# Row maxima with five PSUM banks and a priority of their own, and output tiles completed in turn, in a planned attention and feed-forward kernel

## The chip, the cores and the metric

The kernel runs on one core of one Trainium2 chip. The metric is the device time of one execution in microseconds, given as the median of several runs.

## What is computed

The reference is a decay attention followed by two feed-forward layers, all in float32:

```
B, H, S, D = 4, 8, 576, 64
scores = q @ k.T / 8 + (cum[:, None] - cum[None, :])     # cum = cumsum(log(clip(f, 1e-4, 1)))
scores = where(causal, -1e9, scores)
attn = exp(scores - rowmax(scores)); attn = attn / (sum(attn) + 1e-9)
x = (attn @ v), heads side by side                       # 2304 x 512
h = x @ w_in;  g = h * sigmoid(1.702 * h);                x = g @ w_out     # 512 -> 2048 -> 512
h = x @ w_in2; g = max(h, 0) + alpha * min(h, 0);         out = g @ w_out2  # 512 -> 2048 -> 512
```

## The kernel before, in words

**An order that a planner writes.** The function does not issue instructions directly. It hands operations to a planner (class `Plan`, lines 71 to 178): each with the engines that may run it and an assumed duration on each, the buffers that it reads and writes, and a priority. The method `run` keeps its own clock for every engine, for the SP and ACT DMA queues and for every buffer. In each step it takes, among all operations that can be placed, the one that can start earliest by that clock; among those with the same start the one with the lowest priority number, then the one that ends first, then the one added first:

```
if best is None or (t, o.pri, end, o.seq) < best[0]:
    best = ((t, o.pri, end, o.seq), o, eng, port)
```

The instructions are then issued in this order. On the chip each engine works through its own list in order, so an instruction whose operand is late holds up all that is behind it on that engine.

**Buffers.** A `Pool` has a number of slots, and an operation that writes a new buffer cannot be placed before a slot is free. All eight PSUM banks are one shared set (`all_banks`); each use of PSUM has a pool with a limit on how many of them it may hold at once (lines 307 to 311):

- `ps_s`, 4: attention scores. Each key tile takes two, one for each of two heads.
- `ps_m`, 2: the score tiles from which row maxima are taken, and the bank that transposes the maxima.
- `ps_v`, 3: the attention outputs. Each unit takes two.
- `ps_h` and `ps_y`, 2 each: hidden layer and output of the feed-forward blocks that run beside attention. `ps_h2` and `ps_y2`, 4 each, serve the later blocks.

**Attention** is cut into 32 units: two heads of one batch and one of two ranges of query rows (0 to 256, then 256 to 576). First come the 16 units of the first range, then the 16 of the second. A unit i has three parts.

- `prep` (line 500) loads k, q and v, transposes k and q on DVE (L518) and splits them into a high and a low part (L354 or L356, L359). Its priority is 100 + i - 2, so the preparation of unit i+2 has the priority 100 + i.
- `chunk` (line 572) finds the row maxima. For every tile of 128 query rows it multiplies q and k for each head (L602; the last 64 rows go by L595 and L596), adds the mask and takes the maximum on DVE (L611), merges two maxima for the last rows (L618), turns the maxima with a matmul against the identity (L627) and writes them with a minus sign into DQ (L636 on ACT or L638 on DVE). Priority 100 + i.
- `chunk2` (line 643) computes the scores again, key tile by key tile, in four products for each head. The last of them (DQ with DK) subtracts the maximum and adds the decay (L663). Then come the exponential on ACT (L667), the triangle on POOL (L671) and the product with the values (L683, L689, or L712 with split operands), and at the end the normalisation: L722 or L725, L728, L731, L732, L742. Priority 100 + i. It is added to the plan after `chunk` of the next unit.

The units of the first range have two key tiles, those of the second five.

**Feed-forward beside attention.** As soon as 256 columns of the attention output are there, `mlp1a` (line 776) runs the first 8 of 16 slices of the first layer on them (L755, L761, L762, L797), with priority 1000 and more, as filler for PE. The weights are split numbers that are put together on ACT, DVE and POOL first (`convert`, L475 to L489).

**Later blocks.** After attention the other 8 slices run in blocks of 512 columns (L755, L878), then the second layer (L755, L766, L769, L907) in five blocks, the last with 512 rows. A slot of the second layer first makes the hidden slice, splits it into gh and gl, and then adds the products for all four output tiles of 128 rows: gh for the four tiles (eight matmuls), then gl for the four tiles (four matmuls). After the last slot each tile is copied out of PSUM into a `qyp` buffer, of which there are two, and stored (L916, L921):

```
for t in range(nt):
    yo = Buf(q_yp)
    plan.add([("ACT", ...), ("DVE", ...)], ... copy(e, yo.ap, py[t].ap), [py[t]], [yo], base)
```

The copies show up under the lines of the helper, L354 and L356. `q_xb` is a pool of two buffers of the same shape, into which the blocks' inputs are loaded (`load_x`, line 857).

Of the kernel before, what the change touches and what calls it, by code (L numbers as in the profile page):

```python
# [181 lines left out]
def kernel(  # L182
# [20 lines left out]
    NP = H // 2  # L203
    KT = DM // P
    NM = DFF // P
# [12 lines left out]
    A0 = 100.0  # L218
    plan = Plan()
# [82 lines left out]
    def psum_pool(cap):  # L302
        p = Pool(cap, (), all_banks)
        p.make = lambda i: banks[i]
        return p

    ps_s = psum_pool(4)
    ps_m = psum_pool(2)
    ps_v = psum_pool(3)
    ps_h = psum_pool(2)  # L310
    ps_y = psum_pool(2)

# [5 lines left out]
    q_xb = sb("b1", "qxb", 2, [P, 512], F32, after_att)  # L318
    q_yp = sb("b1", "qyp", 2, [P, 512], F32, after_att)
# [23 lines left out]
    def c_dve(n, fast=False):  # L343
        return n / (1.92 if fast else 0.96) + 68.0

    def c_act(n, ps=False):
        return n / 1.2 + (51.0 if ps else 93.0)
# [56 lines left out]
    for nm, p, view, n, val in (  # L404
# [8 lines left out]
        for i in range(p.n):  # L413
            b = fill[nm, i] = Buf()
# [16 lines left out]
    for part, (lo, hi) in enumerate(((0, SPLIT), (SPLIT, S))):  # L431
        ts_ = [t for t in range(NKT) if lo <= t * P < hi]
        pri = -80 if part == 0 else A0 + 4.5
# [63 lines left out]
    W1, W2 = {}, {}  # L497
# [67 lines left out]
    def col0(b, q0):  # L565
        return b * SPLIT if q0 == 0 else B * SPLIT + b * (S - SPLIT)


    def c_mm(n, m=P):
        return max(0.4375 * n + 7.0, 111.0 if m > 64 else 57.0)  # L570

    def chunk(u, q0, q1, pri):
        kh, dk, qh, dq, z = u["kh"], u["dk"], u["qh"], u["dq"], u["z"]
        mx = Buf(p_mx)
        fmx = filled("mx", p_mx)
# [2 lines left out]
        nt = len(tiles)  # L578
# [45 lines left out]
        for i0 in range(0, len(jobs), 4):  # L624
# [5 lines left out]
            for i, (j, t, a, w, hhs) in enumerate(jb):  # L630
                for g, hh in enumerate(hhs):
# [6 lines left out]
                            nc.vector.tensor_scalar_mul(d, s_, -1.0)  # L638

                    plan.add([("ACT", 280.0), ("DVE", 240.0)], ev, [(pt, i0), *u["fdq"]], [(dq, ("x", i0 + i, hh))], pri)  # L640
        return dict(u=u, q0=q0, q1=q1, pri=pri)

    def chunk2(x):
        u, q0, q1, pri = x["u"], x["q0"], x["q1"], x["pri"]
# [182 lines left out]
    pend = []  # L827
    for i, (b, hp, q0, q1) in enumerate(seq):
        unit = prep(b, hp, q0, q1, A0 + i - PRE, i < EARLY, 2 <= i < ACTQ)
        pend.append((chunk(unit, q0, q1, A0 + i), col0(b, q0) + q1 - q0 if hp == NP - 1 else 0))  # L830
        if i == NP:
            for m in range(NA):
                W1[m] = weight(wA, w1_in, w1_out, m, A0 + 4 + m * 0.6, A0 + 1 + m if m < 2 else None)
        if len(pend) > 1:
            x, t = pend.pop(0)
            chunk2(x)
            advance(t, 0)
# [7 lines left out]
    blocks = []  # L845
# [21 lines left out]
    for i, (t0, n) in enumerate(blocks):  # L867
        base = 3000.0 + 100 * i
        rd = [(b_xs, c) for c in range(t0 // BLK, (t0 + n) // BLK)]
        xh, xl, rx = load_x(xscr, rd, t0, n, base - 150)  # L870
        py = [Buf(ps_y2) for _ in range(KT)]
        for m in range(NA, NM):
            gh, gl = mlp_slot(W1[m], xh, xl, rx, n, ps_h2, q_g, "swish", m, base + m, base + m - 50)

            def ymm(e, i_, m=m, gh=gh, gl=gl, py=py, n=n):
                for d in range(KT):
                    for a, g in ((0, gh), (1, gh)) if i_ == 0 else ((0, gl),):
                        nc.tensor.matmul(  # L878
                            py[d].ap[:, :n], W1[m].ap[:, a, KT + d, :], g.ap[:, :n],
                            start=(m == NA and i_ == 0 and a == 0), stop=(m == NM - 1 and i_ == 1),  # L880
                        )
# [13 lines left out]
    for i, (t0, n) in enumerate(blocks):  # L895
        base = 4000.0 + 100 * i
        xh, xl, rx = load_x(y1scr, [(b_y1, (i, d)) for d in range(KT)], t0, n, base - 150)
        nt = n // P
        py = [Buf(ps_y2) for _ in range(nt)]
        for m in range(NM):  # L900
            gh, gl = mlp_slot(W2[m], xh, xl, rx, n, ps_h2, q_g, "prelu", m, base + m, base + m - 50)

            def ymm(e, i_, m=m, gh=gh, gl=gl, py=py, nt=nt):
                wo = W2[m].ap.rearrange("p a c n -> p a (c n)")
                for t in range(nt):
                    for a, g in ((0, gh), (1, gh)) if i_ == 0 else ((0, gl),):
                        nc.tensor.matmul(  # L907
                            py[t].ap, g.ap[:, t * P:(t + 1) * P], wo[:, a, KT * P:],
                            start=(m == 0 and i_ == 0 and a == 0), stop=(m == NM - 1 and i_ == 1),
                        )  # L910

            plan.add([("PE", 2 * nt * c_mm(512))], lambda e, ymm=ymm: ymm(e, 0), [(W2[m], (1, 0)), (W2[m], (1, 1)), gh], py, base + m)
            plan.add([("PE", nt * c_mm(512))], lambda e, ymm=ymm: ymm(e, 1), [(W2[m], (1, 0)), gl], py, base + m)
        for t in range(nt):
            yo = Buf(q_yp)
            plan.add([("ACT", c_act(512, True)), ("DVE", c_dve(512))], lambda e, t=t, yo=yo, py=py: copy(e, yo.ap, py[t].ap), [py[t]], [yo], base)  # L916
            x = t0 + t * P
            while x < t0 + (t + 1) * P:
                r, y = row_of(x)
                y = min(y, t0 + (t + 1) * P)  # L920
                plan.add(DMA((y - x) * 2048), lambda e, x=x, y=y, r=r, yo=yo, o=x - t0 - t * P: nc.sync.dma_start(  # L921
                    out[r:r + y - x, :], yo.ap[o:o + y - x, :]
                ), [yo], (), base)
                x = y
# [37 lines left out]
```

## Time and profile before

| | |
|---|---|
| median of 3 runs | 1076.21 us (1075.81 to 1078.11) |
| the profiled execution | 1075.87 us, span 1074.1 us |
| PE matmul busy | 1033.8 us, 96% of the span |
| PE weight load busy | 886.3 us, 83% |
| DVE busy | 690.3 us, 64% |
| ACT busy | 447.9 us, 42% |
| POOL busy | 125.5 us, 12% |
| DMA | 86.55 MB, mean 81 GB/s |

Times count from the start of the span. PE, DVE, ACT, POOL and SP are the engines. A row of the timeline gives the start, the duration, the engine, the line of the kernel, what is written from what, and how many instructions were merged; in square brackets stands how long the engine had been idle and what ended that. An arrow points from the one who waited to what it waited for. Attention ends at about 418 us, and the feed-forward work beside it at about 480 us.

### The profile page before, as it was taken

To read this page: it belongs to the slowest core of one execution; us is meant where nothing else is said; L and a number is where in the kernel's file an instruction comes from. 1 tells how busy PE (TensorE), PEld (TensorE's weight loads), DVE (VectorE), ACT (ScalarE), POOL (GpSimd) and SP (SyncE) were. 2 spreads that over 40 slices of the span, in tenths; PEclk is the share of its full clock that TensorE was granted. 3 is DMA by queue.
4 is the path that set the end of the run, shared out by engine and by line. 5 is a ranking of instruction groups with operands and counts; after the bars stand their busy time and mean duration, and the time that the engine had idled before them with its cause. 6 is when DMAs were issued, how large, how long until landed. Compare 5 with 4: busy or idle time off the path is not lost.

```text
span 1074.1 us, 17787 instructions
## 1 busy us (share of the span) xinstructions
PE 1033.8 (96%) x6531; PEld 886.3 (83%) x6531; DVE 690.3 (64%) x1565; ACT 447.9 (42%) x1042; POOL 125.5 (12%) x192
## 2 busy tenths in 40 slices
PE   5868999999999899999999999999999999999997
PEld 3656888889998789998878898888888888898885
DVE  5879987888878877959963359734343533534433
ACT  4557554665555565847742247301211201211101
POOL 6223221211111111002100101200000000000000
PEclk7789999999999999999999999999999999999999
DMA  5577563333242111645742235300200200000001
GB/s 110 120 172 183 128 154 73 67 78 66 48 92 41 52 24 60 215 140 175 227 159 88 79 118 177 118 1 1 69 1 1 69 0 1 33 28 20 1 1 39
DMA packets 170056, 86.55 MB, mean 81 GB/s; under 512 B 127440, under 2 KB 155280, under 8 KB 169968
## 3 DMA queue, kind: packets, MB, share of 16 engines
q1 hardware_dynamic: 160720, 84.30, 28.8%
q10 hardware_dynamic: 9248, 1.12, 0.7%
q8 instruction: 51, 0.84, 0.3%
q14 instruction: 37, 0.30, 0.1%
HBM read 66.34 MB, written 19.02 MB: 79 GB/s over the span
## 4 chain that ended last, share of the span: by engine, by line
PE 51%; DVE 3%; DMA 2%; ACT 1%; issue 0%; SPq 0%; DVEq 0%; ACTq 0%
PE bk L755 26%; PE bk L907 18%; PE bk L878 6%; DMA wraw<-in_moe_w_out_dram 1%; PE bk L797 1%; DVE wraw L484 1%; DVE wA L359 1%; DVE wc L487 0%; DVE qgg L762 0%; ACT wraw L480 0%; DVE qgl L359 0%; ACT wc L479 0%; DMA qxb<-xscr 0%; DVE wc L481 0%; DMA out_dram<-qyp 0%
## 5 line engine op out<-in xcount | busy, mean ns | idle before, releaser
L354 ACT CAST qgh<-qgg 128x512 fp32r<-128x512 f32 (+1 forms) x118 | 68.2, 578 | 334.3 <-DVE qgg L769 297.3
L766 DVE TENSOR_SCALAR qgg<-bk,alpha_sb 128x512 f32<-128x512 f32 (+1 forms) x80 | 55.4, 694 | 164.9 <-PE bk L755 164.9
L755 PE MATMUL bk<-qx,wB 128*128 128x512 f32 (+1 forms) x720 | 155.8, 368 | 0.0
L755 PEld LDWEIGHTS bk<-qx,wB 128*128 128x128 f32 x720 | 125.9, 189 | 22.7
L755 PE MATMUL bk<-xh,wA 128*128 128x256 f32 x576 | 120.6, 292 | 0.0
L359 DVE TENSOR_TENSOR qgl<-qgg,qgh 128x512 fp32r<-128x512 f32 (+1 forms) x117 | 74.8, 641 | 68.8 <-ACT qgh L354 52.2
L755 PE MATMUL bk<-qx,wA 128*128 128x512 f32 (+1 forms) x480 | 103.6, 368 | 0.0
L755 PEld LDWEIGHTS bk<-xh,wA 128*128 128x128 f32 x576 | 95.3, 192 | 7.0 <-issue 4.0
L755 PEld LDWEIGHTS bk<-qx,wA 128*128 128x128 f32 x480 | 84.2, 188 | 15.3
L797 PE MATMUL bk<-gh,wA 128*128 128x256 f32 x576 | 82.9, 287 | 3.9 <-ACT gh L354 3.2
L755 PE MATMUL bk<-xl,wA 128*128 128x256 f32 x288 | 81.9, 284 | 1.1 <-DVE xl L359 1.1
L611 DVE CUSTOM_DVE_ANT_0 bk<-bk,mask 128x512 f32<-128x512 f32 (+3 forms) x160 | 75.2, 492 | 10.1 <-PE bk L602 8.3
L797 PEld LDWEIGHTS bk<-gh,wA 128*128 128x128 f32 x576 | 73.8, 191 | 7.6 <-ACT gh L354 3.9
L667 ACT ACTIVATE e<-bk 128x320 f32<-128x320 f32 (+3 forms) x224 | 66.5, 364 | 22.4 <-PE bk L663 21.4
L907 PE MATMUL bk<-wA,qgh 128*128 128x512 f32 x288 | 71.9, 389 | 0.0
L907 PEld LDWEIGHTS bk<-wA,qgh 128*128 128x128 f32 x288 | 53.8, 188 | 11.0
L671 POOL TENSOR_SCALAR_AFFINE_SELECT e<-e 128x256 f32<-128x256 f32 (+1 forms) x80 | 33.6, 432 | 208.4 <-ACT e L667 180.6
L755 PEld LDWEIGHTS bk<-xl,wA 128*128 128x128 f32 x288 | 55.4, 192 | 1.4 <-DVE xl L359 1.3
L878 PE MATMUL bk<-qgh,wB 128*128 128x512 f32 (+1 forms) x240 | 54.3, 368 | 0.8 <-ACT qgh L354 0.8
L907 PE MATMUL bk<-wB,qgh 128*128 128x512 f32 x216 | 53.9, 390 | 0.0
L479 ACT ACTIVATE wc<-wraw 128x512 f32<-128x512 f32 x64 | 43.1, 678 | 24.3 <-DMA wraw<-in_moe_w_out_dram 11.8
L755 PE MATMUL bk<-qx,wC 128*128 128x512 f32 (+1 forms) x240 | 52.8, 368 | 0.0
(154 smaller groups left out, 2038.4 us busy)
## 6 DMA issues: line engine op xcount, KB each, us to landing
wraw<-in_moe_w_in_dram SPq DMA_DIRECT2D x32, 512.0 KB
wraw<-in_moe_w_out_dram SPq DMA_DIRECT2D x32, 512.0 KB
xscr<-xr SPq DMA_DIRECT2D x9, 512.0 KB
ypscr<-yp SPq DMA_DIRECT2D x18, 256.0 KB
rk<-in_k_dram SPq DMA_DIRECT2D x64, 72.0 KB
VR<-in_v_dram SPq DMA_DIRECT2D x32, 128.0 KB
qxb<-xscr SPq DMA_DIRECT2D x16, 256.0 KB
qyp<-ypscr SPq DMA_DIRECT2D x16, 256.0 KB
```

The costliest lines, as they stand in the source:

```text
L354: nc.scalar.copy(dst, src)
L359: E[e].tensor_tensor(dst, a, b, op=ALU.subtract)
L479: plan.add([("ACT", c_act(n))], lambda e: nc.scalar.mul(w.ap, high().bitcast(F32), 2.0 ** -112), [raw], [w], pri)
L484: lambda e: nc.vector.scalar_tensor_tensor(low(), high(), -2 ** 31, low(), op0=ALU.bitwise_and, op1=ALU.bitwise_or),
L611: plan.add([("DVE", c_dve(c1 - c0) + 90.0)], lambda e, pm=pm, c0=c0, c1=c1, mk=mk, m0=m0, col=col: nc.vector.tensor_tensor_reduce(pm.ap[:, ...
L667: plan.add([("ACT", c_act(m, True))], lambda e, hh=hh, pss=pss, e32=e32, w=w, m=m: nc.scalar.activation(e32.ap[:w, hh, :m], pss[hh].ap[:w, ...
L671: plan.add([("POOL", 150.0 + 0.82 * 2 * w, 0.0, True)], lambda e, e32=e32, w=w: nc.gpsimd.affine_select(e32.ap[:w, :, :w], e32.ap[:w, :, : ...
L755: nc.tensor.matmul(ph.ap[:, :n], wb.ap[:, a, c, :], x(c), start=(c == 0 and i == 0), stop=(c == KT - 1 and i == 2))
L766: plan.add([("DVE", c_dve(n) + 56)], lambda e: nc.vector.tensor_scalar(g.ap[:, :n], ph.ap[:, :n], 0.0, alpha_sb[:, m:m + 1], op0=ALU.min, ...
L797: nc.tensor.matmul(py[d // 2].ap[:, d % 2 * BLK:(d % 2 + 1) * BLK], W1[m].ap[:, a, KT + d, :], g.ap, start=(m == 0 and i == 0 and a == 0 a ...
L878: nc.tensor.matmul(py[d].ap[:, :n], W1[m].ap[:, a, KT + d, :], g.ap[:, :n], start=(m == NA and i_ == 0 and a == 0), stop=(m == NM - 1 and ...
L907: nc.tensor.matmul(py[t].ap, g.ap[:, t * P:(t + 1) * P], wo[:, a, KT * P:], start=(m == 0 and i_ == 0 and a == 0), stop=(m == NM - 1 and i ...
```

## The change

Three things change.

- The limits on PSUM banks: scores 4 to 2, maxima 2 to 5, attention outputs 3 to 4. The eight banks stay shared.
- The operations of `chunk` get the priority 100 + i - 0.5 instead of 100 + i. `chunk2` and `prep` keep theirs.
- In the last slot of the last block the products of the output tiles are separate operations: gh for tiles 0 and 1, gl for tile 0, gl for tile 1, then gh and gl for tile 2, then gh and gl for tile 3, each with a slightly higher priority number than the one before. Tiles 1 and 3 of that block are copied into `qxb` buffers, tiles 0 and 2 into `qyp` buffers.

```diff
-    ps_s = psum_pool(4)
-    ps_m = psum_pool(2)
-    ps_v = psum_pool(3)
+    ps_s = psum_pool(2)
+    ps_m = psum_pool(5)
+    ps_v = psum_pool(4)
...
-    def chunk(u, q0, q1, pri):
+    def chunk(u, q0, q1, upri, pri):
...
-        return dict(u=u, q0=q0, q1=q1, pri=pri)
+        return dict(u=u, q0=q0, q1=q1, pri=upri)
...
-        pend.append((chunk(unit, q0, q1, A0 + i), ...))
+        pend.append((chunk(unit, q0, q1, A0 + i, A0 + i - 0.5), ...))
...
-            def ymm(e, i_, m=m, gh=gh, gl=gl, py=py, nt=nt):
+            def ymm(e, i_, m=m, gh=gh, gl=gl, py=py, ts_=range(nt)):
...
-                for t in range(nt):
+                for t in ts_:
...
-            plan.add([("PE", 2 * nt * c_mm(512))], lambda e, ymm=ymm: ymm(e, 0), [(W2[m], (1, 0)), (W2[m], (1, 1)), gh], py, base + m)
-            plan.add([("PE", nt * c_mm(512))], lambda e, ymm=ymm: ymm(e, 1), [(W2[m], (1, 0)), gl], py, base + m)
+            last = i == len(blocks) - 1 and m == NM - 1
+            for ts_ in (range(0, 2), range(2, 3), range(3, nt)) if last else (range(nt),):
+                k_ = len(ts_)
+                py_ = [py[t] for t in ts_]
+                plan.add([("PE", 2 * k_ * c_mm(512))], lambda e, ymm=ymm, ts_=ts_: ymm(e, 0, ts_=ts_), [(W2[m], (1, 0)), (W2[m], (1, 1)), gh], py_, base + m + 0.01 * ts_[0])
+                for t2 in ([t] for t in ts_) if last else (ts_,):
+                    plan.add([("PE", len(t2) * c_mm(512))], lambda e, ymm=ymm, t2=t2: ymm(e, 1, ts_=t2), [(W2[m], (1, 0)), gl], [py[t] for t in t2], base + m + 0.01 * t2[0])
         for t in range(nt):
-            yo = Buf(q_yp)
+            yo = Buf(q_xb if last and t % 2 else q_yp)
```

## Rows read from the trace of the kernel before

**Rows 1.** The page: engine totals, and PE's busy share in 40 slices.

```profile
PE 1033.8 (96%) x6531; PEld 886.3 (83%) x6531; DVE 690.3 (64%) x1565; ACT 447.9 (42%) x1042; POOL 125.5 (12%) x192
...
PE   5868999999999899999999999999999999999997
```

**Rows 2.** Windows: length, busy PE, PEld, DVE, ACT, POOL; PEclk, DMA share, GB/s.

```profile
10.00:70.00 60.00, 42.71 (x302) 34.55 (x303) 44.41 (x150) 28.24 (x75) 19.94 (x32) 0.69 0.60 133
70.00:110.00 40.00, 34.05 (x296) 27.40 (x294) 38.38 (x110) 32.51 (x82) 12.47 (x17) 1.00 0.73 187
110.00:350.00 240.00, 239.71 (x2113) 213.04 (x2110) 200.93 (x553) 134.37 (x385) 40.65 (x68) 1.00 0.38 81
350.00:400.00 50.00, 46.82 (x401) 40.98 (x400) 40.52 (x112) 27.66 (x80) 5.89 (x11) 0.97 0.15 41
400.00:1060.00 660.00, 658.84 (x3384) 562.90 (x3383) 359.02 (x627) 215.99 (x411) 37.63 (x33) 1.00 0.23 72
```

**Rows 3.** Waits of PE over the whole span: total us, times, longest us.

```profile
PE bk L663 <- DVE DQ L638: 6.4, 1, 6.4
...
PE bk L627 <- DVE MX L611: 4.2, 1, 4.2
...
PE bk L627 <- DVE MX L618: 2.5, 2, 2.2
PE bk L663 <- ACT e L667: 2.4, 3, 1.5
...
PE bk L602 <- DVE MX L611: 0.8, 1, 0.8
```

**Rows 4.** Timeline of the end; last row: the output stores, ns min/median/max.

```profile
1063.53 0.69 DVE L359 TENSOR_TENSOR qgl<-qgg,qgh 128x512 fp32r<-128x512 f32 x1 [0.76 <-ACT qgh L354]
...
1063.68 1.98 PE L907 MATMUL bk<-wC,qgh 128*128 128x512 f32 x8
...
1065.49 1.07 PE L907 MATMUL bk<-wC,qgl 128*128 128x512 f32 x4
1065.92 0.59 ACT L354 COPY qyp<-bk 128x512 f32<-128x512 f32 x1 [2.43 <-PE bk L907]
...
1066.53 4.36 SPq L921 DMA_DIRECT2D out_dram<-qyp x5
1068.65 0.59 ACT L354 COPY qyp<-bk 128x512 f32<-128x512 f32 x1 [2.14 <-DMA out_dram<-qyp]
1069.95 0.59 ACT L354 COPY qyp<-bk 128x512 f32<-128x512 f32 x1 [0.71 <-DMA out_dram<-qyp]
...
L921 SPq DMA_DIRECT2D out_dram<-qyp x5: 333/338/587, 1066.5 to 1070.6; - x5
```

**Rows 5.** Timeline of 365 to 369 us, three operations of DVE.

```profile
365.68 0.51 DVE L518 STREAM_TRANSPOSE tq<-rq 128x320 f32<-128x320 f32 x1
...
367.73 0.77 DVE L518 STREAM_TRANSPOSE tk<-rk 128x576 f32<-128x576 f32 x1
...
368.52 0.10 DVE L618 TENSOR_TENSOR MX<-MX 128x1 fp32r<-128x1 f32 x1
```

**Rows 6.** Timeline of 14 to 15 us, DVE ahead of the first maxima.

```profile
14.71 0.51 DVE L462 CAST xr<-xr 32x320 fp32r<-32x320 f32 x1 [3.04 <-ACT xr L461]
```

**Rows 7.** Timeline of 62 to 64 us, ACT.

```profile
62.74 0.66 ACT L479 ACTIVATE wc<-wraw 128x512 f32<-128x512 f32 x1 [4.09 <-DMA wraw<-in_moe_w_in_dram]
...
63.97 0.27 ACT L636 ACTIVATE DQ<-bk 3x128 fp32r<-3x128 f32 x1
```

**Rows 8.** Timeline of 39 to 41 us: scores of two key tiles, exponentials.

```profile
39.17 0.33 PE L663 MATMUL bk<-QH,KH 64*128 64x256 f32 x2
...
39.69 0.28 PE L663 MATMUL bk<-QH,KH 64*128 64x128 f32 x1
...
39.98 1.19 ACT L667 ACTIVATE e<-bk 128x256 f32<-128x256 f32 x4 [0.15 <-PE bk L663]
```

**Rows 9.** Groups of PE's instructions, 10 to 110 us: busy us, mean ns | idle before.

```profile
L627 PE MATMUL bk<-ident_r,MX 128*99 128x128 f32 x10 | 3.4, 336 | 4.7 <-DVE MX L611 4.2 <-DVE sm L728 0.5
```

More of the change, by code (lines that the diff above doesn't have):

```diff
@@ L829 @@
         unit = prep(b, hp, q0, q1, A0 + i - PRE, i < EARLY, 2 <= i < ACTQ)
-        pend.append((chunk(unit, q0, q1, A0 + i), col0(b, q0) + q1 - q0 if hp == NP - 1 else 0))
+        pend.append((chunk(unit, q0, q1, A0 + i, A0 + i - 0.5), col0(b, q0) + q1 - q0 if hp == NP - 1 else 0))
         if i == NP:
```

## The prediction

> **What bounds the kernel now.** I read the page's engine totals and slices first. TensorE (PE) is busy 96% of the span, and its row is low in two places only: the first four slices and the last [rows 1]. The table of windows puts numbers on that [rows 2]. From 110 to 350 us PE is busy for 239.71 of 240 us, and from 400 to 1060 us for 658.84 of 660. There only shorter matmul work would help, and the change removes no matmul. PE is idle for 17.3 us of the stretch 10 to 70, 6.0 of 70 to 110 and 3.2 of 350 to 400. From 70 to 110 VectorE (DVE) is busy for 38.4 of 40 us, so DVE bounds there and a better order can give almost nothing. From 10 to 70 DVE idles for 15.6 us (60 less 44.41): the room for a better order is there, at 350 to 400, and at the end.
>
> The PE waits say what is late in those places [rows 3]: a DQ operand once for 6.4 us, row maxima (MX) for 4.2, 2.5 and 0.8 us, the exponentials for 2.4 us. In the last microseconds PE has finished, and the copies of the output tiles wait for DMAs [rows 4].
>
> **The change, part by part.**
>
> *Last output tiles.* Now the last slot issues eight gh matmuls at 1063.68 and four gl matmuls at 1065.49, and PE ends at about 1066.5. The first copy starts at 1065.92. The third starts only at 1068.65 and the fourth at 1069.95, because the two qyp buffers come free when the DMAs of the first two have landed; the SP queue's five issues therefore end at 1066.53 + 4.36 = 1070.89 [rows 4]. Afterwards the same twelve matmuls run by tile (eight start in the 1.81 us from 1063.68 to 1065.49, 0.226 us each, 2.7 us over twelve), and every tile has a buffer of its own, two qyp and two qxb; the last reads of qxb, by this block's splitting, are long over. The gl of tile 0 is wanted at 1063.68 + 4 x 0.226 = 1064.6, and qgl is ready at 1063.53 + 0.69 = 1064.2, so that reordering exposes no wait; were qgl 0.4 us later, PE would wait for the difference. Tiles then finish at about 1065.05, 1065.3, 1066.0 and 1066.6. The last copy takes 0.59 us and its issue 0.34, so the last issue ends at about 1067.6 instead of 1070.89. SP's other four issues, 0.33 to 0.59 us each, fit between 1065.7 and 1067.3. I take **-3.2 us**. The bounds are -3.4 (no queueing on SP) and -2.6 (the last copy is on DVE and its issue queues behind another).
>
> *Priority of the row maxima.* The planner starts whatever can start earliest, and priority decides only between operations that could start at the same instant. Half a step puts the maxima of unit i ahead of the preparation of unit i+2, which ties with them now, but not ahead of the products of unit i-1. The clearest instance is at 366 to 369 us: the merge of two maxima (L618) runs at 368.52, after the transposes of tq (0.51 us) and tk (0.77 us) of a later unit [rows 5], and PE waits 2.2 of the 2.5 us for it. With those two behind the maxima, 1.3 us go. I add the 0.8 us that PE waits in L602 for L611, which free banks remove, and 0.4 us for smaller ones of the kind: **-2.5 us**, between 0 (start times differ, so priority never decides) and -3.7 (all waits on MX but the 4.2). The 4.2 us stays: there the first maxima stood behind L462 on DVE, which had itself waited 3.04 us for ScalarE (ACT) [rows 6], and no bank or tie is involved. No DMA is issued by the maxima, so the loads keep their place in SP's queue; the preparation that falls behind has two units of lead, which hides it, and if that lead were gone it would cost its two transposes, 1.3 us, per unit.
>
> *The order as a whole is redrawn.* Any edit to the planner changes which operation stands ahead of which on each engine. The 6.4 us stall is such a case: ACT has a weight conversion (L479) queued ahead of the DQ evictions, its load comes 4.09 us late, and L636 follows at 63.97 [rows 7]; DQ, then PE, wait. The new priority does not aim at this pair, since that conversion already ranks behind the unit. After a redraw the stall may stay, go, or fall elsewhere. Bounds are -6.4 and +6.4 (a second one like it); I take half of it going, **-3.2 us**, because it is much the longest wait of the run, the other PE waits being 4.2 and less.
>
> *Four banks for the outputs instead of three.* The next unit's value products no longer wait for the previous unit's normalisation. No wait of PE on that is in the list, so 0, with a gain of at most the 2.4 us on exponentials as bound.
>
> *Two banks for scores instead of four.* This is what the change gives away. Now the second tile's scores start at 39.69, before the first tile's exponentials have begun at 39.98; the four exponentials run back to back in 1.19 us [rows 8]. With two banks the second pair of scores waits for the first two exponentials, about two thirds of that (256 columns against 128), which makes the unit's chain some 0.75 us longer. PE runs in order; behind the waiting scores stand the next unit's maxima and the feed-forward matmuls, which the planner can place ahead of them. So a handover costs nothing where such work is at hand (110 to 350 us) and up to 0.75 us where it is not. There are 16 handovers in the first half (one per unit) and 64 in the second. Ten units have their maxima transposed between 10 and 110 us [rows 9]. Short of filler are the first half of them, five units, and one unit's four handovers near 360 to 374: nine, so 0 to +6.8 us. The maxima of the next unit lie between, so I take nearer the low end, **+2.0 us**.
>
> In the Trainium skill, "Perfetto Trace Analysis", Optimizing Tensor Performance, independent matmul groups should rotate through different PSUM banks so that evacuation of one overlaps the matmuls of the next. It speaks for the maxima and against the scores here, and by it alone the handover would be exposed throughout; that is the slower rival below. The row of the second scores agrees with the rule, for they do overlap the first tile's evacuation now.
>
> **Sum.** -3.2 - 2.5 - 3.2 + 2.0 = -6.9 us. The profiled execution took 1075.87 us (a span of 1074.1 and 1.8 around it), 0.34 below the median of 1076.21. So 1075.87 - 6.9 = 1069.0 for such an execution, and 1069.3 against the median. About 0.2% (2.2 us) is what a measurement of this kernel can tell from no change.
>
> **Rivals.**
>
> *The early stage packs better as a whole.* The DVE idle time from 10 to 70 us is 15.6 us; less the 3.0 us behind L462, 12.6 us could be had, and 3.2 us at 350 to 400. For it: PE has gaps for many small reasons there, and five banks let a unit's maxima all be issued at once. Against: DVE is full right behind it, so work pulled forward soon meets that limit. With a bit over half, 10 us, and the end's 3.2: 1063. With all of it: 1076.2 - 12.6 - 3.2 - 3.2 = 1057.
>
> *Only the end counts.* Start times decide and ties are rare, so the priority does little; the redrawn order brings as many stalls as it removes. For it: PE is full for most of the stretch whatever the order. That gives 1076.2 - 3.2 = 1073.
>
> *Scores wait for exponentials (slower).* The place is the scores of each tile but the first, the price 0.75 us each. If 15 of the 80 handovers are exposed in place of nine partly hidden ones, and the large stall stays: -3.2 - 2.5 + 11.2 = +5.5, or 1082. It decides (slower by 0.2%) from 11 exposed handovers on: (2.2 + 5.7)/0.75. For it: ten units run before 110 us, where the feed-forward work is not always ready; maxima that hold five of eight banks can keep scores and feed-forward from starting. Against: PE has filler for 240 us on end.
>
> **How the numbers follow.** Forecast, 1066 to 1072: 0.40. Early stage better, under 1066: 0.17. Only the end, 1072 to 1075: 0.22. Slower stage, over 1075: 0.21. Faster by over 0.2% means below 1074.1: 0.40 + 0.17 + 0.18 of the third = 0.75. Slower means above 1078.4: 0.12 of the last. Between: 0.04 + 0.09 = 0.13. The range runs from the whole-room case, 1057, to 1080, inside the slower case; about 0.05 is left out below and 0.08 above.
>
> **What would show it.** Right: the four last copies follow each other without a wait on out_dram and the span ends about 3.2 us after the last issue; no PE wait on L618 of over 1 us; at most half of the wait on L638 left; feed-forward proper starting some 4 us earlier, with its length as before. Wrong: new PE waits in L663 on the exponentials of more than 5 us, or PE idle before 110 us at 23 us or over. The forecast fails upward if 10 to 110 us has more PE idle than now, and downward if 10 to 70 us loses over half of its DVE idle time.

## The result and the profile after

The changed kernel takes 1089.22 us (median of 4 runs, 1084.91 to 1090.77) against 1077.16 of the kernel before beside it: a ratio of 1.0095, with an interval of 1.0078 to 1.0112. It is slower by 12 us; 6.9 us less were forecast. The profiled execution took 1089.67 us, its span is 1087.9.

The page of the changed kernel, engine totals and PE's 40 slices:

```profile
PE 1054.6 (97%) x6531; PEld 889.5 (82%) x6531; DVE 683.7 (63%) x1558; ACT 455.9 (42%) x1035; POOL 147.0 (14%) x206
...
PE   5798999999999999999999999999999999999998
```

PE does the same 6531 matmuls, is busy 20.8 us longer and has fewer gaps than in [rows 1]. By its busy share nothing is wrong. The windows of the changed kernel (columns as in [rows 2]) show what is:

```profile
10.00:70.00 60.00, 48.39 (x340) 36.95 (x339) 43.41 (x155) 30.88 (x89) 22.20 (x37) 0.68 0.60 128
70.00:110.00 40.00, 33.81 (x248) 28.21 (x248) 37.30 (x97) 29.50 (x69) 6.63 (x10) 0.89 0.66 183
110.00:350.00 240.00, 236.63 (x1994) 195.08 (x1990) 201.05 (x578) 140.80 (x383) 64.28 (x89) 1.00 0.39 82
350.00:400.00 50.00, 50.00 (x421) 43.23 (x420) 34.65 (x94) 26.34 (x72) 8.47 (x14) 1.00 0.12 33
400.00:1060.00 660.00, 657.70 (x3425) 565.04 (x3424) 354.60 (x612) 218.06 (x412) 36.50 (x25) 1.00 0.23 73
```

Up to 110 us the two are level: 340 + 248 = 588 matmuls here, 302 + 296 = 598 in [rows 2]. Then, from 110 to 350 us, PE starts 1994 matmuls where it started 2113, at a granted clock of 1.00 (2.4 GHz) both times. These 119 matmuls, at 240 us / 2113 = 0.114 us, are 13.5 us, about the whole loss. That is an estimate: the matmuls differ in size, and the redraw e5 below starts only 2058 there and still takes 1077.74 us. The busy time of PE fell by only 3.1 us there, because the recorded durations of matmuls overlap, and a delay of 0.1 us lies inside them. Two groups of the changed kernel show how far (busy us, mean ns of one):

```profile
L907 PE MATMUL bk<-wA,qgh 128*128 128x512 f32 x288 | 72.0, 390 | 0.0
L907 PEld LDWEIGHTS bk<-wA,qgh 128*128 128x128 f32 x288 | 53.7, 188 | 11.2 <-ACT qgh L354 0.3
```

288 matmuls of 390 ns would be 112 us, and are 72.0 busy; the weight loads, 288 x 188 ns = 54, don't overlap. So these show the loss: 213.04 us busy before, 195.08 after, in the same 240 us. The work left over comes later: 20 more matmuls in 350 to 400, 41 more behind.

Attention itself isn't late. The last product of its last unit and the first product of the later blocks (L878), before and then after:

```profile
419.19 0.45 PE L683 MATMUL bk<-e,VR 64*64 64x64 f32 x8
...
480.32 1.98 PE L878 MATMUL bk<-qgh,wB 128*128 128x512 f32 x8
```

```profile
403.57 0.45 PE L683 MATMUL bk<-e,VR 64*64 64x64 f32 x8
...
492.12 2.00 PE L878 MATMUL bk<-qgh,wB 128*128 128x512 f32 x8
```

Attention ends 15.6 us earlier, and the later blocks begin 11.8 us later. So it is the feed-forward work beside attention that was put off.

Waits of PE after the change:

```profile
PE bk L627 <- DVE MX L611: 6.4, 4, 4.4
...
PE bk L683 <- POOL e L671: 3.3, 3, 2.0
PE bk L755 <- ACT DQ L636: 3.2, 2, 2.4
...
PE bk L663 <- ACT e L667: 0.7, 2, 0.4
```

The wait of 6.4 us on DQ [rows 3] is gone, so is the one on L618. The scores wait for the exponentials for 0.7 us only, less than the 2.4 before. It is the exponentials that wait for PE. The group of L667 in the changed kernel (busy us, mean ns | idle before, and what ended it), then in the kernel before:

```profile
L667 ACT ACTIVATE e<-bk 128x320 f32<-128x320 f32 (+3 forms) x224 | 68.8, 357 | 64.9 <-PE bk L663 60.4 <-POOL e L671 1.9 <-issue 1.8
```

```profile
L667 ACT ACTIVATE e<-bk 128x320 f32<-128x320 f32 (+3 forms) x224 | 66.5, 364 | 22.4 <-PE bk L663 21.4 <-issue 0.3
```

What PE does in the stretch of the loss is seen in its timeline. First the changed kernel, 270.75 to 273.17 us:

```profile
270.75 0.42 PE L663 MATMUL bk<-QH,KH 64*128 64x320 f32 x2
271.00 0.31 PE L663 MATMUL bk<-QL,KH 64*128 64x320 f32 x2
271.15 0.31 PE L663 MATMUL bk<-QH,KL 64*128 64x320 f32 x2
271.30 0.31 PE L663 MATMUL bk<-DQ,DK 64*128 64x320 f32 x2
271.53 0.56 PE L712 MATMUL bk<-eh,VH 128*128 128x320 f32 x2
271.93 0.45 PE L712 MATMUL bk<-eh,VL 128*64 128x320 f32 x2
272.22 0.45 PE L712 MATMUL bk<-el,VH 128*128 128x320 f32 x2
272.61 0.41 PE L663 MATMUL bk<-QH,KH 64*128 64x320 f32 x2
272.86 0.31 PE L663 MATMUL bk<-QL,KH 64*128 64x320 f32 x2
```

The same value product (L712) in the kernel before, among feed-forward matmuls:

```profile
261.17 0.28 PE L755 MATMUL bk<-xh,wA 128*128 128x256 f32 x1
261.28 0.46 PE L712 MATMUL bk<-eh,VH 128*128 128x320 f32 x2
261.58 0.45 PE L712 MATMUL bk<-eh,VL 128*64 128x320 f32 x2
261.87 0.45 PE L712 MATMUL bk<-el,VH 128*128 128x320 f32 x2
262.16 0.81 PE L689 MATMUL bk<-e,VR 128*128 128x192 f32 x4
```

Scores and most row maxima (L663, L602) use 64 rows of the array (`64*128`, rows and columns), the rest almost all 128. Among 128-row neighbours the six matmuls of L712 take 262.16 - 261.28 = 0.88 us. Between two groups of scores they take 272.61 - 271.53 = 1.08: the first pair 0.40 and not 0.30, the last 0.39 and not 0.29. The scores lose almost as much on their side: 0.25 and 0.23 us from pair to pair at the ends and 0.15 inside, so 0.18 us. No wait is recorded on these rows. (One of 0.1 us would lie inside the overlapping durations and wouldn't show; h1 below has no such wait to hide.) And in these microseconds PE alternates between the two kinds with no feed-forward work between: that block's first layer has begun at 229.70, but its second layer only starts at 279.59, 50 us later; before, the block's two came at 204.03 and 228.17. (The kernel before has one such wait as well, 49.7 us in its seventh block.)

So there were two readings: the alternation itself costs the time, or the feed-forward blocks are starved of banks and PE lacks filler. And since a planner redraws its order at any edit, a third: the order was bad luck.

### The profile page after: what moved, and what is told of

It is laid out like the page before. It is cut to its first block, busy times and chain, and to the rows that moved or that the text cites. A ratio compares the mean times of both kernels' runs of the same rounds, so it can differ in the third digit from the quotient of the medians.

```text
span 1087.9 us, 17791 instructions
## 1 busy us (share of the span) xinstructions
PE 1054.6 (97%) x6531; PEld 889.5 (82%) x6531; DVE 683.7 (63%) x1558; ACT 455.9 (42%) x1035; POOL 147.0 (14%) x206
## 4 chain that ended last, share of the span: by engine, by line
PE 82%; DVE 6%; DMA 5%; ACT 3%; issue 2%; SPq 1%; ACTq 0%; POOL 0%; DVEq 0%; POOLq 0%
PE bk L755 33%; PE bk L907 18%; PE bk L797 9%; PE bk L878 6%; PE bk L663 6%; PE bk L712 4%; PE bk L683 2%; PE bk L602 2%; DMA wraw<-in_moe_w_in_dram 2%; DMA wraw<-in_moe_w_out_dram 1%; PE bk L689 1%; DMA rq<-in_q_dram 1%; DVE bk L611 1%; DMA VR<-in_v_dram 1%; DVE wraw L484 1%
## 5 line engine op out<-in xcount | busy, mean ns | idle before, releaser
L755 PE MATMUL bk<-xh,wA 128*128 128x256 f32 x576 | 124.8, 296 | 4.5 <-ACT DQ L636 3.2
L755 PEld LDWEIGHTS bk<-xh,wA 128*128 128x128 f32 x576 | 97.7, 196 | 12.5 <-issue 4.1
L667 ACT ACTIVATE e<-bk 128x320 f32<-128x320 f32 (+3 forms) x224 | 68.8, 357 | 64.9 <-PE bk L663 60.4
L611 DVE CUSTOM_DVE_ANT_0 bk<-bk,mask 128x512 f32<-128x512 f32 (+4 forms) x160 | 74.9, 492 | 7.5 <-PE bk L602 3.2
L797 PEld LDWEIGHTS bk<-gh,wA 128*128 128x128 f32 x576 | 76.2, 196 | 3.7 <-issue 2.0
L671 POOL TENSOR_SCALAR_AFFINE_SELECT e<-e 128x256 f32<-128x256 f32 (+1 forms) x80 | 38.1, 480 | 172.0 <-ACT e L667 167.8
L359 POOL TENSOR_TENSOR qx<-qxb,qx 128x512 fp32r<-128x512 f32 (+1 forms) x9 | 14.2, 1582 | 321.7 <-ACT qx L354 293.3
L878 PE MATMUL bk<-qgh,wB 128*128 128x512 f32 (+1 forms) x240 | 54.6, 369 | 1.7 <-ACT qgh L354 1.7
```

Of the source, the lines that this page charges most:

```text
L359: E[e].tensor_tensor(dst, a, b, op=ALU.subtract)
L611: plan.add([("DVE", c_dve(c1 - c0) + 90.0)], lambda e, pm=pm, c0=c0, c1=c1, mk=mk, m0=m0, col=col: nc.vector.tensor_tensor_reduce(pm.ap[:, ...
L667: plan.add([("ACT", c_act(m, True))], lambda e, hh=hh, pss=pss, e32=e32, w=w, m=m: nc.scalar.activation(e32.ap[:w, hh, :m], pss[hh].ap[:w, ...
L671: plan.add([("POOL", 150.0 + 0.82 * 2 * w, 0.0, True)], lambda e, e32=e32, w=w: nc.gpsimd.affine_select(e32.ap[:w, :, :w], e32.ap[:w, :, : ...
L755: nc.tensor.matmul(ph.ap[:, :n], wb.ap[:, a, c, :], x(c), start=(c == 0 and i == 0), stop=(c == KT - 1 and i == 2))
L797: nc.tensor.matmul(py[d // 2].ap[:, d % 2 * BLK:(d % 2 + 1) * BLK], W1[m].ap[:, a, KT + d, :], g.ap, start=(m == 0 and i == 0 and a == 0 a ...
```

## The experiments

Every kernel below but the one before has the new treatment of the last tiles, so that this part is the same in all of them. For each, beside the time, I worked out from the matmul records how late each matmul of the first 500 us starts against the point to which those ahead of it keep PE. How long a matmul keeps PE is an assumption: its columns at 2.4 GHz, four times that for the plain float32 products, half for the products that run in pairs on 64 rows, a small floor for short ones. With two passes in place of four the columns of lateness come out higher, but kernels with the old and with new limits stay apart at changes. This lateness is split in two: that of the first matmul behind a change between three kinds, the 64-row kind (L602, L663), the products of L683 (64 columns of the array) and all others ("at changes"), and all the rest ("elsewhere"). A wait that falls on a change counts there too.

| kernel | score, maxima, output banks; priority | median us | against before | changes | late at changes | elsewhere |
|---|---|---|---|---|---|---|
| before | 4, 2, 3; old | 1077.16 | | 237 | 24.1 | 59.0 |
| after | 2, 5, 4; new | 1089.22 | 1.0095 | 321 | 36.7 | 60.5 |
| e1 end only | 4, 2, 3; old | 1074.69 | 0.9967 | 237 | 24.3 | 60.5 |
| e2, 231 ns | 4, 2, 3; old | 1094.60 | 1.0145 | 242 | 27.8 | 74.9 |
| e5, 228 ns | 4, 2, 3; old | 1077.74 | 1.0004 | 238 | 24.3 | 62.7 |
| e6, 234 ns | 4, 2, 3; old | 1076.75 | 1.0001 | 249 | 24.4 | 63.0 |
| f1 priority only | 4, 2, 3; new | 1072.60 | 0.9961 | 241 | 24.5 | 56.4 |
| f2 maxima alone | 4, 5, 3; old | 1089.72 | 1.0109 | 257 | 32.1 | 64.2 |
| g4, f2 at 228 ns | 4, 5, 3; old | 1083.81 | 1.0049 | 282 | 32.3 | 58.7 |
| f3 scores alone | 2, 2, 3; old | 1088.71 | 1.0107 | 292 | 33.0 | 67.7 |
| f4 no fifth bank | 2, 2, 4; new | 1086.54 | 1.0082 | 308 | 36.2 | 58.0 |
| e3 four for scores | 4, 5, 4; new | 1088.93 | 1.0100 | 301 | 38.3 | 57.4 |
| e4 old priority | 2, 5, 4; old | 1092.77 | 1.0142 | 329 | 41.0 | 57.5 |
| e8, after at 228 ns | 2, 5, 4; new | 1114.47 | 1.0325 | 320 | 42.2 | 78.0 |
| g1 two banks kept | 2, 5, 4; new | 1087.09 | 1.0095 | 324 | 34.3 | 62.1 |
| g2, g1 at 228 ns | 2, 5, 4; new | 1093.95 | 1.0160 | 322 | 34.9 | 67.1 |
| g3, e1 with them kept | 4, 2, 3; old | 1100.34 | 1.0223 | 254 | 34.0 | 78.6 |

### The parts of the change

**e1** takes the last tiles alone: the kernel before with the new `ymm` operations and `q_xb` copies of the diff above, and nothing else.

> The kernel before with nothing but the last output tiles completed in turn; the rest of the order is the same instruction for instruction. The prediction's own term for this part is -3.2 us (bounds -2.6 to -3.4), whichever theory holds for the attention stage: near 1073 against 1076. If the copies do not wait any more but the last stores queue behind each other, -1 to -2.

It took 1074.69 us beside 1077.82: a ratio of 0.9967 (0.9951 to 0.9984), or -3.1 us; -3.2 was the term. The end of the changed kernel, which has the same edit:

```profile
1080.13 1.07 PE L907 MATMUL bk<-wC,qgh 128*128 128x512 f32 x4
...
1082.37 0.59 ACT L354 COPY qyp<-bk 128x512 f32<-128x512 f32 x1 [0.32 <-PE bk L907]
...
1083.05 0.58 ACT L354 COPY qxb<-bk 128x512 f32<-128x512 f32 x1
1083.71 0.54 SPq L927 DMA_DIRECT2D out_dram<-qyp  x1
1084.34 0.39 SPq L927 DMA_DIRECT2D out_dram<-qxb  x1
```

No copy waits for a store any more, and from the first gh matmul to the end of the last issue it is 1084.73 - 1080.13 = 4.60 us (4.62 in e1), 7.21 in [rows 4]. The gain in the trace is 2.6, the low bound, since SP issues back to back and the last copy, done at 1083.63, gets its issue at 1084.34.

**e3** gives the scores their four banks back, **e4** takes the priority back, both from the changed kernel:

```diff
-    ps_s = psum_pool(2)
+    ps_s = psum_pool(4)
```

> The changed kernel with four banks for scores again (four, five, four). Theory: the 13 us of slowing and the 3 us that the end should have won come from scores waiting for exponentials, so this runs within 4 us of the end alone, and ACT's idle time before L667 that PE's L663 ends falls from 60 us to about 20. Rival (five banks for maxima, or the priority, crowd the others out): it stays 10 us or more above the end alone. Lucky draw: the same, 10 us or more above.

```diff
-        pend.append((chunk(unit, q0, q1, A0 + i, A0 + i - 0.5), ...))
+        pend.append((chunk(unit, q0, q1, A0 + i, A0 + i), ...))
```

> The changed kernel with the maxima at their old priority (two, five, four banks and the new end). Theory (scores): as slow as the changed kernel, within 4 us, ACT's wait for L663 still at 50 us or more. Rival (the priority puts the maxima ahead of the preparation and starves what comes after): most of the 16 us come back.

Neither brings the time back: 1.0100 (1.0067 to 1.0133) and 1.0142 (1.0116 to 1.0168). So the loss doesn't hang on the two score banks alone, and the old priority doesn't cure it.

**f1** adds only the priority to e1, **f2** only five banks for maxima, **f3** only two for scores; **f4** is the changed kernel with two for maxima.

```diff
f1  chunk(unit, q0, q1, A0 + i, A0 + i - 0.5)
f2  ps_m = psum_pool(5)
f3  ps_s = psum_pool(2)
f4  ps_m = psum_pool(2)
```

> Old limits (four, two, three), new priority, new end. Theory (the limits cost, the priority does not): 1072 to 1079, as three of the four draws with the old limits were, and a matmul count between 110 and 350 us near 2100. If the priority is the cause: 1085 or more and a count under 2000.

> Five banks for maxima, the rest old (four, five, three, old priority), new end. Theory A (maxima that may hold five banks keep the scores from starting): 1085 or more, ACT waiting over 40 us for L663 ahead of the exponentials, under 2010 matmuls from 110 to 350 us. Rival (the score limit is the cause): 1072 to 1079 and under 30 us of that wait.

> Two banks for scores, the rest old (two, two, three, old priority), new end. Rival (the score limit): 1083 or more, over 40 us of ACT waiting for L663. Theory A (maxima): 1072 to 1080, with at most the two or three microseconds that the prediction put on the handovers.

> The changed kernel with two banks for maxima again (two, two, four, new priority, new end). Theory A: back to 1072 to 1080. Rival (scores, or four banks for outputs): still 1083 or more.

f1: 0.9961 (0.9942 to 0.9980), f2: 1.0109 (1.0080 to 1.0138), f3: 1.0107 (1.0079 to 1.0135), f4: 1.0082 (1.0058 to 1.0106). Each new limit alone is 14 to 15 us longer than e1, in one draw each, and the two don't add up. The 110 to 350 us row of f2, then of f3:

```profile
110.00:350.00 240.00, 233.93 (x2006) 197.20 (x2005) 203.66 (x581) 139.33 (x394) 58.94 (x87) 0.99 0.39 83
```

```profile
110.00:350.00 240.00, 238.92 (x2055) 206.77 (x2056) 194.03 (x543) 135.68 (x373) 51.87 (x74) 1.00 0.39 82
```

e1 starts 2112 matmuls there. With either new limit PE falls back in the same stretch as after the whole change, though with five banks for maxima it also idles there, for 6.1 us.

### How much a redraw moves

`LAT`, the time that the planner allows between an operation and those that use its result, is 230 ns. One or a few nanoseconds more change no instruction, but the order comes out another. **e2**, **e5** and **e6** are e1 with another value, **e8** the changed kernel. The changed kernel at 231 ns (**e7**), which was to stand beside e2, has no time: with that value the planner comes to a point at which no operation can be placed.

```diff
-LAT = 230
+LAT = 231      # e2; 228 in e5 and e8, 234 in e6
```

> As the end alone, but the planner's assumed latency between engines is 231 ns in place of 230: an edit that means nothing and redraws the order of the whole attention stage. Theory (two score banks make the scores wait): within 4 us of the end alone, because the bank limits are those of before. Rival (the order before was a lucky draw, and any redraw loses): about 10 to 16 us slower than the end alone, as the change is.

> The end alone with an assumed latency of 228 ns: a second meaningless redraw with the old bank limits and priority. If the order of before is a lucky draw: 1085 to 1097, like the first redraw (1094.6). If the first redraw was an unlucky one: within 4 us of the end alone, 1071 to 1079.

> The end alone with 234 ns: a third redraw with the old limits. Lucky draw: 1085 to 1097. Unlucky first redraw: 1071 to 1079.

> The changed kernel with 228 ns: a second redraw with the new limits. Limits: 1085 or more, with over 270 places where PE changes its line behind a wait between 110 and 420 us. Draw alone: anywhere from 1075 to 1097.

e2 is 1.0145 (1.0116 to 1.0173), e5 1.0004 (0.9989 to 1.0019), e6 1.0001 (0.9980 to 1.0021), e8 1.0325 (1.0283 to 1.0368). One nanosecond costs 20 us, two on the changed kernel 25. In e2 the row from 110 to 350 us and the longest wait are:

```profile
110.00:350.00 240.00, 235.54 (x2054) 207.22 (x2051) 194.68 (x541) 129.54 (x368) 47.40 (x78) 0.99 0.39 84
```

```profile
PE bk L797 <- ACT gh L354: 14.8, 4, 6.1
```

So a single comparison of two orders can't tell an edit of a few microseconds from luck. Many can. Of the five kernels with e1's edit, the old limits and eight shared banks (e1, e2, e5, e6, f1) four take 1072.6 to 1077.7 us and one 1094.6; of the ten with a new limit none is under 1083.8. And the table says where: the four orders with the old limits and the old priority after e1's edit lose 24.3 to 27.8 us at changes, f1 24.5, while those that differ by `LAT` alone differ elsewhere (60.5, 62.7, 63.0, 74.9). With any of the new limits, whatever the draw, it is 32 to 42 at changes, and elsewhere nearly the same spread as with the old ones. (g3, with two banks kept, has 34.0 with the old limits.) More lateness at changes goes with the limits; 14 of the 20 us that e2 loses against e1, and 15 of the 37 that e8 loses against e5, lie elsewhere.

### Filler for PE

**g1** tests starvation: two of the eight banks are kept for `ps_y`, the outputs of the feed-forward blocks beside attention, until the ninth block has given its two back. **g2** is g1 at 228 ns, **g3** does this to e1, **g4** is f2 at 228 ns.

```diff
+    self.heir = None
...
+                    if p.heir is not None and p.gone == 2 * 9:
+                        p.heir.free.extend(p.free)
+                        p.heir.free.sort()
+                        p.free.clear()
...
-    all_banks = Pool(8)
+    all_banks = Pool(6)
...
-    ps_y = psum_pool(2)
+    ps_y = Pool(2)
+    ps_y.free = [(0.0, 6), (0.0, 7)]
+    ps_y.make = lambda i: banks[i]
+    ps_y.heir = all_banks
```

> The changed kernel, but two of the eight banks belong to the feed-forward outputs (L797) alone until the last of the nine blocks is done; attention and the hidden slices share the other six, with the new limits and the new priority. Theory (starved filler: attention holds all the banks that L797 needs two of, so PE runs out of feed-forward work in the middle): blocks 2 to 5 begin L797 within about 25 us of their first L755 (in the changed kernel 26, 50, 35, 26), and the time falls from 1089 to 1080 or less. Rival (the new limits cost through the order of attention itself): 1086 or more.

> The same with 228 ns, the draw that took 1114 us with the new limits and all eight banks shared (first L797 of blocks 2 to 4 after 34, 54 and 58 us). Starved filler: at least 20 us come back, 1094 or less, and no block waits over 30 us. Rival: over 1100.

> The end alone (old limits and priority) with the same two banks set apart. Starved filler: the old limits leave the feed-forward its banks mostly already, so within 5 us of the end alone, 1070 to 1080. Rival (any edit that leaves six banks to attention costs): 1085 or more.

> Five banks for maxima alone (four, five, three, old priority, new end) with 228 ns, a second draw of that limit. If the limit costs whatever the draw: 1085 or more, with first L797 of blocks 2 to 4 over 30 us after the first L755 (31, 46, 41 in the first draw for blocks 1 to 3). If the first draw was chance: near 1078, as the old limits are with 228 ns.

In g1 the wait between a block's first and second layer falls from 25 to 50 us (the second to the sixth of the nine blocks; the expectation counts from 0) to between 5 and 18, so starvation was real and is gone. But the time is 1087.09, a ratio of 1.0095 (1.0067 to 1.0122), as without the banks kept. The row from 110 to 350 us of g1:

```profile
110.00:350.00 240.00, 236.44 (x2014) 199.90 (x2014) 193.01 (x548) 135.99 (x377) 66.41 (x89) 1.00 0.39 82
```

2014 matmuls and 324 changes: filler was there, and PE changes as often as without. g2 is 1.0160 (1.0127 to 1.0192), 20 us better than e8, 11 of them elsewhere in the table (67.1 against 78.0), 7 at changes (34.9 against 42.2). By the mark set beforehand, 1094 or less, that speaks for starvation in e8's draw. On the old limits the same edit is a loss, 1.0223 (1.0188 to 1.0259), 25.7 us against e1, where at most 5 were expected: it has a price of its own there. So g1 shows that starvation isn't what raises the number of changes; whether it costs the changed kernel something beside, g1 can't tell, since a gain and the price of the kept banks may cancel. g4 is 1.0049 (1.0028 to 1.0071): five banks for maxima cost 6 us against e5, which has the old limits at the same 228 ns, and 15 in f2's draw. That lies between the two forecasts, 1085 or more and near 1078.

### The price of a change

**h1** measures the alternation by itself, far from attention: e1 with 80 extra matmuls in the last layer, each a product with 64 columns of zeros, so that the sums stay what they are. In 40 slots the extra one has 128 rows, in 40 only 64.

```diff
+    zero = const.tile([P, 64], F32R, name="zero")
...
+        nc.gpsimd.memset(zero.bitcast(F32), 0.0)
...
+                    if i_ == 0 and t == 1:
+                        k = 64 if m % 2 else P
+                        nc.tensor.matmul(py[t].ap[:, 0:64], gh.ap[0:k, 0:P], zero[0:k, :], start=False, stop=False)
```

> The end alone with 80 extra matmuls in the second layer, one in the middle of each slot's eight gh products; each adds a product of gh with 64 zero columns to the output tile, so the sums are unchanged. In even slots it uses all 128 rows, in odd slots rows 0 to 63; the order is otherwise the same. Theory (PE pays for changing between 64-row and full matmuls, about 0.1 us or more a change, with no wait on any engine): in odd slots the stretch around the extra matmul is at least 0.15 us longer than in even slots, so 40 x 0.15 = 6 us or more of the whole. Rival (changes cost nothing by themselves, only late operands do): even and odd slots cost the same 0.03 to 0.06 us each, 2 to 5 us in all.

Two slots of it in PE's timeline, one of each sort:

```profile
700.23 1.07 PE L909 MATMUL bk<-wA,qgh 128*128 128x512 f32 x4
701.13 0.19 PE L915 MATMUL bk<-zero,qgh 128*128 128x64 f32 x1
701.16 1.17 PE L909 MATMUL bk<-wA,qgh 128*128 128x512 f32 x4
702.17 1.08 PE L909 MATMUL bk<-wA,qgl 128*128 128x512 f32 x4
...
707.17 1.07 PE L909 MATMUL bk<-wA,qgh 128*128 128x512 f32 x4
708.17 0.29 PE L915 MATMUL bk<-zero,qgh 64*128 64x64 f32 x1
708.39 1.18 PE L909 MATMUL bk<-wA,qgh 128*128 128x512 f32 x4
709.41 1.07 PE L909 MATMUL bk<-wA,qgl 128*128 128x512 f32 x4
```

From the first gh matmul to the first of gl it is 1.94 us with the 128-row matmul and 2.24 with the 64-row one; without either it is 1.81 [rows 4]. The smaller product costs 0.43 us, the larger one 0.13. It stands between two changes; if it costs no more by itself than the larger one, a change costs 0.15 us, and no wait is recorded. The 128-row product, too, costs more than the 0.03 to 0.06 us that I had put on it. In sum 40 x (0.43 + 0.13) = 22 us, and h1 took 1096.11, 21.4 more than e1 (1.0162 against before, 1.0146 to 1.0179). Where the time goes is seen in the group of the weight loads:

```profile
L915 PEld LDWEIGHTS bk<-zero,qgh 128*128 128x128 f32 x40 | 7.5, 188 | 1.5
L915 PEld LDWEIGHTS bk<-zero,qgh 64*128 64x128 f32 x40 | 7.3, 183 | 14.2 <-issue 14.2
```

The weight load ahead of a 64-row matmul starts 14.2 / 40 = 0.36 us after the end of the weight load before it, the 128-row one 1.5 / 40 = 0.04. As I read it, it isn't drawn ahead of the running matmuls of the other kind. The changed kernel makes 84 more changes than before in 500 us: 84 x 0.15 = 12.6 us.

The table's own 36.7 - 24.1 = 12.6 is another thing that happens to be as large: it holds waits for operands that fall on a change, and leaves out the second and third matmul behind it, which are late as well. To part the price from the waits I took, in the same reckoning, the delays of up to 0.3 us of the first three matmuls behind a change between the 64-row kind and the others (L683 left aside); there are 171 such changes before and 251 after. In every kernel of the table these delays come to 0.15 to 0.2 us a change, about h1's price. They are 17 to 19 us more in the changed kernel than before (the range is that of four or two passes for the plain float32 products), while the delays of over 0.3 us, wherever they fall, are 4 to 7 us fewer. So the changed kernel did lose waits, and paid more for its changes than it gained. In f3 the short delays are 9 us above e1's. In f2 they are only 2 to 3 us above; most of its 7.8 us more at changes are delays of over 0.3 us, and its 15 us have no single cause that I can name.

**h2** and **h3** try to make use of this: the planner adds 90 ns where PE would go from one kind to the other, in the changed kernel and in f1.

```diff
+                    if eng == "PE" and o.half != half:
+                        t += 90.0
...
+                if eng == "PE":
+                    half = o.half
```

> The changed kernel, whose planner now also counts 90 ns when PE changes between operations of 64-row matmuls and others, so that it places fewer of them: 172 changes in the order of PE in place of 280 (the kernel before has 186). Theory: the 14 us that the changed kernel is behind come back, 1077 or less, with the new limits and the new priority kept. Rival (banks or the wait for exponentials): 1086 or more.

> Old limits, new priority, new end, and the same 90 ns in the planner: 100 changes in place of 190. Theory: 90 changes at 0.1 us less than the same kernel without it (1072.6), 1060 to 1066. Rival: within the spread of the draws with old limits, 1072 to 1095.

There are fewer changes in the table's count of three kinds, 225 in place of 321 and 153 in place of 241, and it is much slower: 1.0423 (1.0401 to 1.0446) and 1.0502 (1.0477 to 1.0527). Window and waits of h3:

```profile
110.00:350.00 240.00, 218.95 (x1780) 195.26 (x1781) 169.73 (x469) 115.92 (x323) 38.45 (x60) 0.91 0.34 73
```

```profile
PE bk L669 <- DVE DQ L644: 9.2, 8, 1.6
PE bk L718 <- DVE el L365: 8.3, 6, 2.5
```

Now PE idles for 21 of the 240 us, and the granted clock, 1.00 before, is 0.91 on the mean of the stretch. As I read the waits, the penalty moves scores and maxima back, attention's chain gets late, and the products stand in PE's list ahead of operands that aren't there. In the table's terms 91.5 and 103.5 us are late elsewhere, the lower clock included, and 40.9 and 33.7 at changes. Here the changes avoided cost more than they saved. That such an order would pay was a miss.

**What is settled and what is open.** That a change between 64-row and 128-row matmuls has a price of 0.15 to 0.2 us, and that the changed kernel pays it some 80 times more, is shown by h1, the timeline and the table; it is enough for its loss. The same goes for most of f3's, but not for f2's, which stays open. How two score banks come to more changes than four is argued, not shown: with two, the planner has to put something between two groups of scores, and with more banks for maxima more small groups are free to start in any gap. It is also open whether the limits help when the number of changes is held, since the one way tried held it by waiting, and what starvation costs by itself. f1 beats both kernels, 5.0 us under the one before; 3.1 of that are the last tiles, and the other 2 are less than a redraw moves.

## Why the prediction was wrong

**Last output tiles: right.** -3.2 was forecast; -3.1 by the times of e1, -2.6 by the trace, the low bound. The last issue does queue on SP, though behind a copy on ACT and not, as the bound had it, on DVE.

**Priority: near in size, not shown.** -2.5 was forecast; f1 is 2.1 us under e1, with 4.1 us less lateness elsewhere. The wait on L618 went in the changed kernel as well, and the 4.2 on the first maxima stayed (4.4). A redraw by one nanosecond moves more than that, so the agreement may be luck.

**The redrawn order: the wrong size.** The term was -3.2, between -6.4 and +6.4, taken from the longest single wait. The stall on DQ did go, in the changed kernel as in f1. But the draws of one and the same kernel span 1074.7 to 1094.6 (e1, e2, e5, e6), and 25 us lie between the changed kernel and e8. The bound should have been three times as wide and mostly upward, since the kernel before is one of the better draws.

**Four banks for outputs at 0: not tried alone.** f4 against f3, which differ by that and the priority, gives -2.2 us, less than a redraw moves.

**Two banks for scores: the wrong size and the wrong mechanism.** The term was +2.0, between 0 and +6.8, for scores that wait for exponentials. f3 measured +14.0 in its one draw, with 8.7 of it at changes; the scores of the changed kernel wait for exponentials for 0.7 us. The slower rival had the sign and named the score banks, but its price, scores that wait for exponentials, didn't occur. What it gave as a reason beside, that maxima with five of eight banks can keep the feed-forward work from starting, did. Five banks for maxima were counted as a gain alone, and cost 6 to 15 us (g4 against e5, f2 against e1).

**The step that failed** is the sentence that from 110 to 350 us, with PE busy 239.71 of 240 us, only shorter matmul work would help and the change removes none. From it the terms took that an order couldn't lose there: a handover "costs nothing where such work is at hand (110 to 350 us)". But a matmul's place in the order sets its price. A busy share of 100% is no proof that PE starts matmuls as fast as it can; 119 fewer start in the same 240 us at a busy time 3.1 us less, and some 80 changes more, at 0.15 to 0.2 us each, are 12 to 16 us that the sum had no term for. The row itself held the better measure: weight loads were busy for 213.04 of 240 us, and fell by 18.0. The Trainium skill says as much in "Perfetto Trace Analysis", Identifying the Most-Contended Engine: matmul busy share is no good measure of how near TensorE is to its limit, and the share of its peak arithmetic and the busy share of weight loads should be read instead. The traces here agree, with 239.71 and 236.63 us of matmuls against 213.04 and 195.08 of weight loads.

The price of a change, too, is foreshadowed in the Trainium skill: "TensorEngine Tiling (Array Packing)", Key Properties, has "Changing tiling mode (not just tile) drains the TensorE". The runs agree that a change costs, 0.15 us in h1; that a drain is the reason they don't show. The prediction should have counted the changes in the order of before and made a rival of more of them.

**Most of the signs that it named were the wrong ones.** It would have failed upward if PE idled more than before from 10 to 110 us: PE idles for 17.8 us (100 less 48.39 and 33.81), 23.2 before, though in part at a lower clock, 0.89 from 70 to 110. It asked for waits of L663 on the exponentials of over 5 us: there are 0.7. These looked right while the loss lay in the stretch that it had set aside. One sign did tell: the later blocks were to start some 4 us earlier, and start 11.8 us later.

## What to carry to other kernels

Where a list scheduler writes the order, redraw it by a meaningless edit several times, before and after, ahead of crediting a change of a per cent. Judge whether PE is full by the weight loads' busy time or the matmuls started in a stretch, not by matmul busy time, and both only roughly, since matmuls differ in size. Ask when the stage behind begins. Count how often the order goes from 64-row to 128-row matmuls and back, and price each; but look at what fewer changes cost in later operands.

## What the hardware showed that I had not expected

A change between a 64-row and a 128-row matmul costs 0.15 us with no wait recorded on it, so that a product of 64 rows and 64 columns takes 0.43 us in a 128-row stream where one twice as large takes 0.13. In attention, where the scores of two heads run in pairs on 64 rows each, the rows above give 0.20 us on the side of a six-matmul value product and 0.18 on that of the scores, 0.19 for each of the two changes. The first matmul behind such a change is late by 0.10 us in the median, before and after alike.
